# Weight-sum additions moved to VectorE, their splits and the second pair's factors rescheduled

## The chip, the cores and the metric

The kernel runs on one core of a Trainium2 chip. Its time is the device time of one execution in microseconds (us); the times shown are medians of several runs. Beside each timed kernel there is one execution taken by the hardware profiler, and every row in this document comes from such a profile. The engines are TensorE (PE, with its weight loads PEld), VectorE (DVE), ScalarE (ACT), GpSimd (POOL) and SyncE (SP), which issues nearly all transfers between HBM and the on-chip memory. Each engine works through its own queue in order, and an instruction that waits holds up all that stand behind it in that queue.

## The reference

Random-feature attention for 4 batches of 8 heads, 576 positions and head width 64, followed by two feed-forward layers:

```python
def phi(x):
    h = einsum('bhsd,md->bhsm', x, omega) - sum(x * x) / 2
    return exp(h - max(h)) / sqrt(128)
q_p, k_p = phi(q * scale), phi(k * scale)
kv, z = einsum('bhsm,bhsd->bhmd', k_p, v), sum(k_p, axis=2)
x = (q_p @ kv) / (q_p @ z + 1e-6)            # 2304 tokens x 512
h = x @ w_in;  x = (h * clip(h + 3, 0, 6) / 6) @ w_out      # first layer, 512 -> 2048 -> 512
h = x @ w2_in; x = (h * sigmoid(1.702 * h)) @ w2_out        # second layer
```

The feed-forward weights arrive as 64-bit floating-point words.

## The kernel before

Each 32-bit operand of a large product is split into a high and a low half (a copy into the matmul's format on one engine, a subtraction on another), and a product is three matmuls: high by high, high by low, low by high.

The program has four stages.

- Attention of batch 0 (0 to some 60 us), with the conversion of the first layer's weights beside it.
- The first layer, one batch of 512 tokens after the other, each in 16 chunks `c` of 128 hidden features (`emit_h`, `emit_o`, two chunks apart). Between a batch's matmuls stand the attention steps of the next batch, called from `side()`. All 32 weight tiles (16 of `w_in`, 16 of `w_out`) are converted during batch 0. `HELD` of them stay on the chip; the others are stored to HBM and fetched again in each of the later three batches, through six buffers `wss`, two chunks ahead (`AHEAD`).
- From batch 1 to the ninth chunk of batch 3 (205 to 505 us) the second layer's weights are converted and summed. The list `late` holds this work for eight pairs `u` of chunks. `convert_1` and `convert_2` make the 32-bit weights `w` of a chunk. The second layer uses a scheme of seven block products in place of eight, for which sums of quarter blocks of the weights are needed. `sums` makes them in place, four additions for `w_in` and four for `w_out` of each pair, and `put_sums` splits eight halves of the blocks into `wsn` tiles (a copy on ScalarE, L216, a subtraction on GpSimd, L217) and stores each tile to HBM (`sums_dram`, `left_dram`).
- The second layer (from 575 us) in two pairs `p` of batches. `h_pair` makes the gated values `g` of 256 hidden features, eight times for a pair; `o_pair` multiplies them with `w_out` in seven products of eight turns `u`. In each turn `halves` splits a value (ScalarE L954, VectorE L955) into one of three `gs` tiles and 12 matmuls follow (L960); `total` adds blocks of `g` on GpSimd (L944 to L950). The factors of the next pair, `x_ops`, are made beside the first pair's `o_pair`: two loads and 14 steps that split a block (ScalarE L636, VectorE L637) and add one on GpSimd (L624 to L630), called from that loop's own `side()`.

What stands where in an engine's queue is not fixed by the order of the code. A scheduler runs through the program ahead of time with its own model of how long each instruction takes. It places an instruction when its inputs and its buffer are there, and the place in the code decides only between instructions that are ready together.

Of the kernel before, what the change touches and what calls it, by code (L numbers as in the profile page):

```python
# [22 lines left out]
def performer_moe_kernel(  # L23
# [34 lines left out]
    HELD = 9  # L58
# [155 lines left out]
    def put_sums(u, kind, t):  # L214
        s = wp.tile([P, 2, 2, DM // 2], F32R, tag="wsn", bufs=2, name="wsn")
        nc.scalar.copy(s[:, :, 0], t)  # L216
        nc.gpsimd.tensor_tensor(out=s[:, :, 1], in0=t, in1=s[:, :, 0].bitcast(F32), op=ALU.subtract)  # L217
        if kind in "abcd":
            to = sums_dram[u, kind]
        else:  # L220
            k = LEFT.index(kind)
            to = left_dram[:, k:k + 2, u].rearrange("p o (s d) -> p o s d", s=2)
        nc.sync.dma_start(out=to, in_=s.bitcast(F32))

    def sums(u, k, step):
        w0, w1 = whole[2 * u][:, k], whole[2 * u + 1][:, k]
        first, second = (("a", "b"), ("c", "d")) if k == 0 else (("11", "12"), ("s4", "s2"))
        if step == 0:
            put_sums(u, first[0], w0)
            put_sums(u, first[1], w1)  # L230
            return
        sub = dict(op=ALU.subtract)
        a11, a22 = w0[:, 0], w1[:, 1]
        a12, a21 = (w0[:, 1], w1[:, 0]) if k == 0 else (w1[:, 0], w0[:, 1])
        nc.gpsimd.tensor_tensor(out=a22, in0=a21, in1=a22, op=ALU.add)
        nc.gpsimd.tensor_tensor(out=a21, in0=a11, in1=a21, **sub)
        nc.gpsimd.tensor_tensor(out=a11, in0=a22, in1=a11, **sub)
        nc.gpsimd.tensor_tensor(out=a12, in0=a12, in1=a11, **sub)  # L238
        put_sums(u, second[0], w1)
        put_sums(u, second[1], w0)  # L240
# [250 lines left out]
    def emit_h(n, c, side):  # L491
        w = ws[0, "i", c].rearrange("p s (k f) -> p s k f", k=NK)
        for i, N in SEGS[n]:
# [26 lines left out]
            if i == n:  # L520
                after_gate()
# [185 lines left out]
    for u in range(NC // 2):  # L707
        late += [
            (True, lambda u=u: convert_next(1, NC + 2 * u + 1, *gate)),
            (True, lambda u=u: convert_next(1, NC + 2 * u + 2, *gate)),  # L710
            (False, lambda u=u: convert_next(2, NC + 2 * u + 1)),
            (False, lambda u=u: convert_next(2, NC + 2 * u + 2)),
        ] + [(False, lambda u=u, k=k, j=j: sums(u, k, j)) for k in range(2) for j in range(2)]
    slots = (B - 2) * NC + PREP
    n_late = [0, 0]

    def before_chunk(n, c):
        n_late[1] = min(len(late), -(-len(late) * ((n - 1) * NC + c + 1) // slots))
        while n_late[0] < n_late[1] and not late[n_late[0]][0]:
            late[n_late[0]][1]()  # L720
            n_late[0] += 1

    def after_gate():
        while n_late[0] < n_late[1]:
            late[n_late[0]][1]()
            n_late[0] += 1
# [27 lines left out]
    def side():  # L754
        pace[1] += 1
        if pace[1] % 2:
            return
# [33 lines left out]
    for u in range(len(units) + LAG):  # L791
        while fetches and fetches[0][0] <= u + AHEAD:
            fetch_w(0, *fetches.pop(0)[1:])
        if u < len(units):
# [21 lines left out]
            if n == B - 1 and c >= PREP:  # L816
                if c == PREP:
# [242 lines left out]
    for p in range(B // 2):  # L1060
        while prep:
            prep.pop(0)()
        for u in range(NC // 2):
            h_pair(p, u)
# [70 lines left out]
```

## Time and profile before

| | |
|---|---|
| median of 3 runs | 961.22 us (959.08 to 962.56) |
| profiled execution, whole | 962.68 us |
| its span, first to last instruction | 960.9 us |
| TensorE busy | 925.2 us (96%) |
| VectorE busy | 617.0 us (64%) |
| ScalarE busy | 481.4 us (50%) |
| GpSimd busy | 410.9 us (43%) |
| moved between HBM and the chip | 211.97 MB |
| mean granted TensorE clock | 0.998 of full speed |

The busy time of an engine is the time in which at least one of its instructions ran. A matmul's end is modelled, so that a short stand of TensorE between two matmuls can hide in it.

### The profile page before, as it was taken

What the parts mean: (1) busy time and instruction counts of PE and PEld (TensorE: products, weight loads), DVE (VectorE), ACT (ScalarE), POOL (GpSimd) and SP (SyncE); (2) the same over time, 40 slices, a digit from 0 to 9 for tenths busy, and PEclk for the clock granted to TensorE, in tenths of its full rate; (3) what the DMA queues carried; (4) which work ended last, traced back from release to release, by engine and by line L of the source; (5) the groups of instructions that cost most, each with busy time, mean ns of one, the idle gap of its engine ahead of it and who ended that gap; (6) DMA issues with size and microseconds to landing.
All of it is one profiled execution on the core that took longest, in us unless ns stands there. A gap on an engine that the chain in (4) does not pass through costs nothing.

```text
span 960.9 us, 16331 instructions
## 1 busy us (share of the span) xinstructions
PE 925.2 (96%) x6238; PEld 788.5 (82%) x6238; DVE 617.0 (64%) x946; ACT 481.4 (50%) x977; POOL 410.9 (43%) x335
## 2 busy tenths in 40 slices
PE   8899999999999999999999999997899999999997
PEld 7777777778877877878888887886899888889997
DVE  6888899588574866656627244439976443477743
ACT  5887676576554765645534234334444232244443
POOL 0122213068564466646654006658822254464400
PEclk9999999999999999999999999999999999999999
DMA  5668678678888687876665247765467555555572
GB/s 176 224 230 282 203 260 308 239 278 304 308 295 288 231 285 275 293 264 211 228 242 175 88 133 252 227 209 189 152 190 227 190 165 171 175 175 163 172 259 88
DMA packets 70558, 211.97 MB, mean 221 GB/s; under 512 B 6992, under 2 KB 12752, under 8 KB 70480
## 3 DMA queue, kind: packets, MB, share of 16 engines
q1 hardware_dynamic: 70320, 210.67, 65.0%
q8 instruction: 49, 0.80, 0.3%
q10 hardware_dynamic: 160, 0.26, 0.1%
q14 instruction: 29, 0.24, 0.1%
HBM read 155.85 MB, written 55.05 MB: 219 GB/s over the span
## 4 chain that ended last, share of the span: by engine, by line
PE 50%; DVE 20%; POOL 10%; ACT 8%; DMA 7%; issue 4%; POOLq 0%; SPq 0%; ACTq 0%; DVEq 0%
PE o L960 16%; PE h L844 15%; PE o L550 6%; PE ps L500 6%; DVE w L202 4%; POOL wsn L217 4%; DMA sumsd<-wsn 3%; DVE gs L955 2%; PE hl L861 2%; POOL w L195 2%; DVE xo L637 2%; DVE wtop L186 2%; ACT wsn L216 2%; DVE gs L517 2%; ACT e L263 2%
## 5 line engine op out<-in xcount | busy, mean ns | idle before, releaser
L960 PE MATMUL o<-wss,gs 128*128 128x256 f32 x1536 | 192.2, 285 | 12.2 <-DVE gs L955 12.1
L960 PEld LDWEIGHTS o<-wss,gs 128*128 128x128 f32 x1536 | 187.8, 192 | 16.9 <-DVE gs L955 16.2
L195 POOL TENSOR_TENSOR w<-w,wpow 128x512 f32<-128x512 f32 x64 | 77.2, 1228 | 201.5 <-DVE wpow L190 128.7
L844 PE MATMUL h<-xo,wss 128*128 128x512 f32 x672 | 160.8, 393 | 0.1
L550 PE MATMUL o<-gs,wss 128*128 128x512 f32 (+1 forms) x660 | 150.5, 375 | 1.5 <-ACT gs L516 1.5
L500 PE MATMUL ps<-x,wss 128*128 128x512 f32 x576 | 146.8, 398 | 5.1 <-DVE ga L512 2.5
L844 PEld LDWEIGHTS h<-xo,wss 128*128 128x128 f32 x672 | 124.1, 188 | 26.7 <-DMA wss<-sumsa 0.5
L955 DVE TENSOR_TENSOR gs<-g,gs 128x512 fp32r<-128x512 f32 x112 | 114.8, 1047 | 46.2 <-ACT gs L954 45.4
L550 PEld LDWEIGHTS o<-gs,wss 128*128 128x128 f32 x660 | 112.2, 188 | 22.5 <-ACT gs L516 2.9
L500 PEld LDWEIGHTS ps<-x,wss 128*128 128x128 f32 x576 | 104.1, 188 | 30.1 <-DVE ga L512 3.2
L954 ACT CAST gs<-g 128x512 fp32r<-128x512 f32 x112 | 69.6, 621 | 94.2 <-PE o L960 87.1
L217 POOL TENSOR_TENSOR wsn<-w,wsn 128x512 fp32r<-128x512 f32 x64 | 89.0, 1395 | 62.4 <-ACT wsn L216 62.4
L885 POOL TENSOR_TENSOR g<-g,c 128x512 f32<-128x512 f32 x48 | 64.2, 1338 | 102.5 <-ACT g L884 101.9
L512 DVE SCALAR_TENSOR_TENSOR ga<-ga,ps 128x512 f32<-128x512 f32 (+1 forms) x80 | 49.7, 628 | 84.5 <-ACT ga L511 84.2
L202 DVE TENSOR_TENSOR w<-w,wtop 128x512 f32<-128x512 f32 x64 | 71.6, 1131 | 21.8 <-POOL w L195 21.3
L216 ACT CAST wsn<-w 128x512 fp32r<-128x512 f32 x64 | 39.7, 624 | 81.2 <-POOL w L238 26.8
L517 DVE TENSOR_TENSOR gs<-ga,gs 128x512 fp32r<-128x512 f32 (+1 forms) x80 | 64.0, 812 | 24.5 <-ACT gs L516 23.7
L511 ACT ACTIVATE ga<-ps,three 128x512 f32<-128x512 f32 (+1 forms) x80 | 51.5, 650 | 47.4 <-PE ps L500 47.3
L263 ACT ACTIVATE e<-ps,mx 128x128 f32<-128x128 f32 x220 | 62.9, 395 | 23.1 <-DVE mx L261 22.9
L884 ACT ACTIVATE g<-c 128x512 f32<-128x512 f32 x48 | 30.4, 633 | 79.8 <-DVE c L877 79.8
L550 PE MATMUL o<-gs,wsh 128*128 128x512 f32 (+1 forms) x300 | 68.9, 376 | 1.2 <-ACT gs L516 1.2
L550 PEld LDWEIGHTS o<-gs,wsh 128*128 128x128 f32 x300 | 51.4, 188 | 11.2 <-ACT gs L516 1.5
(158 smaller groups left out, 1356.0 us busy)
## 6 DMA issues: line engine op xcount, KB each, us to landing
wss<-left SPq DMA_DIRECT2D x64, 512.0 KB, 3.7
wss<-ws0i SPq DMA_DIRECT2D x36, 512.0 KB, 4.5
wss<-ws0o SPq DMA_DIRECT2D x33, 512.0 KB, 4.5
wraw<-in_w_in_dram SPq DMA_DIRECT2D x32, 512.0 KB, 4.9
wraw<-in_w_out_dram SPq DMA_DIRECT2D x32, 512.0 KB, 5.8
left<-wsn SPq DMA_DIRECT2D x32, 512.0 KB, 3.2
wss<-sumsa SPq DMA_DIRECT2D x16, 512.0 KB, 3.3
wss<-sumsd SPq DMA_DIRECT2D x16, 512.0 KB, 4.1
```

Source lines behind the costliest of these rows:

```text
L195: nc.gpsimd.tensor_tensor(out=w[:, cols], in0=w[:, cols], in1=q[:, cols], op=ALU.mult)
L202: nc.vector.tensor_tensor(out=wj, in0=wj, in1=a[:, j * DM:(j + 1) * DM], op=ALU.add)
L217: nc.gpsimd.tensor_tensor(out=s[:, :, 1], in0=t, in1=s[:, :, 0].bitcast(F32), op=ALU.subtract)
L263: act = nc.scalar.activation(out=e[:, r, :], in_=ps[:, r, :], func=AF.Exp, bias=mx[:, r:r + 1])
L500: nc.tensor.matmul(out=ps, lhsT=w[:, wi, kk, :], rhs=x[:, xi, kk, :], start=(m == 0), stop=(m == 3 * NK - 1),)
L517: gate[1] = nc.vector.tensor_tensor(out=s[:, 1, :], in0=g, in1=s[:, 0, :].bitcast(F32), op=ALU.subtract)
L550: nc.tensor.matmul(out=ps[:, e, :], lhsT=w[:, wi, cols], rhs=s[:, gi, :], start=(c == 0 and m == 0 and per == 1), stop=(c == NC - 1 and m ...
L844: nc.tensor.matmul(out=ps, lhsT=s[:, wi, q, :], rhs=xop[q, op][:, xi], start=(first and m == 0), stop=(m == 5), skip_group_check=not first,)
L885: eng.tensor_tensor(out=g, in0=g, in1=src, op=ALU.mult)
L954: nc.scalar.copy(s[:, 0], g)
L955: nc.vector.tensor_tensor(out=s[:, 1], in0=g, in1=s[:, 0].bitcast(F32), op=ALU.subtract)
L960: nc.tensor.matmul(out=out, lhsT=s[:, gi, d * P:(d + 1) * P], rhs=w[:, wi, :], start=(start and m == 0), stop=(stop and m == 2), skip_grou ...
```

## The change

Four things are edited.

- `HELD` goes from 9 to 8. The tiles that stay are now eight of `w_out`; before they were four of `w_in` and five of `w_out`. A third `wsn` tile takes the room.
- `sums` is cut into eight calls per pair, one split each, called one at a time from `side()`; before, they were four calls ahead of a chunk. The order of the eight splits changes with it.
- The four additions of each block go from GpSimd to VectorE.
- In the second layer the second pair's factors are paced over 48 turns, from the seventh on, and the first three splits of `o_pair`'s first product are made inside the last `h_pair`, ahead of its last product.

```diff
-    HELD = 9
+    HELD = 8
...
-    def put_sums(u, kind, t):
-        s = wp.tile([P, 2, 2, DM // 2], F32R, tag="wsn", bufs=2, name="wsn")
+    def put_sums(u, k, i):
+        kind = (("a", "b", "c", "d"), ("11", "12", "s4", "s2"))[k][i]
+        t = whole[2 * u + (i in (1, 2))][:, k]
+        s = wp.tile([P, 2, 2, DM // 2], F32R, tag="wsn", bufs=3, name="wsn")
         nc.scalar.copy(s[:, :, 0], t)
         nc.gpsimd.tensor_tensor(out=s[:, :, 1], in0=t, in1=s[:, :, 0].bitcast(F32), op=ALU.subtract)
...
-        nc.gpsimd.tensor_tensor(out=a22, in0=a21, in1=a22, op=ALU.add)
-        nc.gpsimd.tensor_tensor(out=a21, in0=a11, in1=a21, **sub)
-        nc.gpsimd.tensor_tensor(out=a11, in0=a22, in1=a11, **sub)
-        nc.gpsimd.tensor_tensor(out=a12, in0=a12, in1=a11, **sub)
-        put_sums(u, second[0], w1)
-        put_sums(u, second[1], w0)
+        nc.vector.tensor_tensor(out=a22, in0=a21, in1=a22, op=ALU.add)
+        nc.vector.tensor_tensor(out=a21, in0=a11, in1=a21, op=ALU.subtract)
+        nc.vector.tensor_tensor(out=a11, in0=a22, in1=a11, op=ALU.subtract)
+        nc.vector.tensor_tensor(out=a12, in0=a12, in1=a11, op=ALU.subtract)
+
+    def sums(u, n):
+
+        k, i = ((0, 0), (0, 1), (1, 0), (1, 1), (0, 2), (0, 3), (1, 2), (1, 3))[n]
+        put_sums(u, k, i)
+        if n in (2, 4):
+            add_sums(u, n // 2 - 1)
...
-        ] + [(False, lambda u=u, k=k, j=j: sums(u, k, j)) for k in range(2) for j in range(2)]
+        ] + [("side", lambda u=u, n=n: sums(u, n)) for n in range(8)]
...
         if pace[1] % 2:
+            late_at("side", 1)
             return
...
         gated(3, c22, nc.gpsimd)
+        first_split()
         product(4, "b", 1, b7, False)
...
-                s = halves(gp, SM, quarters(u)[src])
+                s = ready.pop(0) if op == 1 and ready else halves(gp, SM, quarters(u)[src])
...
+    def split_early():
+        ready.extend(halves(gp, SM, gt[u, 0][:, 0]) for u in range(3))
...
-            h_pair(p, u)
+            h_pair(p, u, split_early if u == NC // 2 - 1 else lambda: None)
...
-        wait = [2]
+        turn = [0, len(prep)]
 
         def side():
-            wait[0] -= 1
-            if prep and wait[0] < 0:
+            turn[0] += 1
+            while prep and (turn[0] - 6) * turn[1] > (turn[1] - len(prep)) * 48:
                 prep.pop(0)()
```

Three places show what the scheduler makes of it. The numbers behind a name tell its buffers apart, and the lines of the changed kernel are a few further down the file.

ScalarE before, around the sums of the first pair of chunks (`w_2295` and `w_2309`): L216 is the copy that begins a split, L511 and L516 belong to the first layer's gating, L263 are the attention's exponentials.

```order
L516 CAST gs_2489<-ga_2486 128x512 [waits DVE_49]
L216 CAST wsn_2469<-w_2309 128x2x256 [waits DVE_49,Activation_49]
L511 ACTIVATE ga_2569<-ps_2556,three_86 128x512 [waits PE_49]
L516 CAST gs_2572<-ga_2569 128x512 [waits DVE_49]
L368 COPY kv_2586<-ps_2575 128x65 [waits PE_49]
L216 CAST wsn_2540<-w_2309 128x2x256 [waits DMAHW3_49,Activation_49,Pool_49]
L263 ACTIVATE e_2595<-ps_2588,mx_2596 128x128 [waits DVE_49]
L263 ACTIVATE e_2595<-ps_2588,mx_2596 128x128 x3
L263 ACTIVATE e_2595<-ps_2614,mx_2621 128x128 [waits DVE_49]
L263 ACTIVATE e_2595<-ps_2614,mx_2621 128x128 x3
L216 CAST wsn_2544<-w_2295 128x2x256 [waits DMAHW6_49,Activation_49,Pool_49]
```

ScalarE in the changed kernel, the same place (L218 the copy of a split, L512, L517 and L264 the others).

```order
L517 CAST gs_2491<-ga_2488 128x512 [waits DVE_49]
L218 CAST wsn_2478<-w_2311 128x2x256 [waits DVE_49,Activation_49]
L218 CAST wsn_2508<-w_2297 128x2x256
L512 ACTIVATE ga_2563<-ps_2546,three_86 128x512 [waits PE_49]
L218 CAST wsn_2553<-w_2311 128x2x256 [waits DMAHW4_49,DVE_49,Pool_49]
L517 CAST gs_2566<-ga_2563 128x512 [waits DVE_49]
L369 COPY kv_2580<-ps_2569 128x65 [waits PE_49]
L264 ACTIVATE e_2589<-ps_2582,mx_2590 128x128 [waits DVE_49]
L264 ACTIVATE e_2589<-ps_2582,mx_2590 128x128 x3
L264 ACTIVATE e_2589<-ps_2616,mx_2623 128x128 [waits DVE_49]
L264 ACTIVATE e_2589<-ps_2616,mx_2623 128x128 x2
L218 CAST wsn_2602<-w_2311 128x2x256 [waits DMAHW7_49,Pool_49]
```

Ahead of the two groups of exponentials three copies stand in place of two, and the first two of them back to back.

VectorE before, the same place in the program: L512 and L517 are the gating, L261 the maximum of the attention's features, L312 and L313 a split of its inputs.

```order
L517 TENSOR_TENSOR gs_2489<-ga_2486,gs_2489 128x512 [waits Activation_49]
L512 SCALAR_TENSOR_TENSOR ga_2569<-ga_2569,ps_2556 128x512 [waits Activation_49]
L517 TENSOR_TENSOR gs_2572<-ga_2569,gs_2572 128x512 [waits Activation_49]
L261 TENSOR_REDUCE mx_2596<-ps_2588 128x4 [waits PE_49]
L312 CAST thi_2813<-qk_2770 128x512 [waits PE_49]
L261 TENSOR_REDUCE mx_2621<-ps_2614 128x4 [waits PE_49]
L313 TENSOR_TENSOR tlo_2814<-qk_2770,thi_2813 128x512 [waits DVE_49]
L512 SCALAR_TENSOR_TENSOR ga_2658<-ga_2658,ps_2645 128x512 [waits Activation_49]
L517 TENSOR_TENSOR gs_2661<-ga_2658,gs_2661 128x512 [waits Activation_49]
```

VectorE in the changed kernel (L231 to L234 the additions, L513 and L518 the gating, L262 the maximum).

```order
L518 TENSOR_TENSOR gs_2491<-ga_2488,gs_2491 128x512 [waits Activation_49]
L513 SCALAR_TENSOR_TENSOR ga_2563<-ga_2563,ps_2546 128x512 [waits Activation_49]
L231 TENSOR_TENSOR w_2311<-w_2311 128x256 [waits Pool_49]
L232 TENSOR_TENSOR w_2311<-w_2297,w_2311 128x256 [waits DVE_49]
L233 TENSOR_TENSOR w_2297<-w_2311,w_2297 128x256 [waits DVE_49]
L518 TENSOR_TENSOR gs_2566<-ga_2563,gs_2566 128x512 [waits Activation_49]
L234 TENSOR_TENSOR w_2297<-w_2297 128x256 [waits DVE_49]
L262 TENSOR_REDUCE mx_2590<-ps_2582 128x4 [waits PE_49]
L231 TENSOR_TENSOR w_2311<-w_2297,w_2311 128x256 [waits Pool_49]
L313 CAST thi_2815<-qk_2772 128x512 [waits DMAHW6_49,PE_49]
L262 TENSOR_REDUCE mx_2623<-ps_2616 128x4 [waits PE_49]
L232 TENSOR_TENSOR w_2297<-w_2297 128x256 [waits DVE_49]
```

The additions stand between the gating and the maxima; the first of each four waits for GpSimd, the others for the one before.

VectorE before, at the end of the first pair's last `h_pair` and the start of `o_pair`: L955 are splits of gated values, L637 the second pair's factors, L877 the additions of `h_pair`.

```order
L955 TENSOR_TENSOR gs<-g,gs 128x512
L877 TENSOR_TENSOR c_7000<-u_6963,h 128x512
L637 TENSOR_TENSOR xo<-xr,xo 128x512 x4
L877 TENSOR_TENSOR c_7015<-u_6963,h 128x512
L955 TENSOR_TENSOR gs<-g,gs 128x512
L637 TENSOR_TENSOR xo<-xr,xo 128x512
L955 TENSOR_TENSOR gs<-g,gs 128x512 x2
L637 TENSOR_TENSOR xo<-xr,xo 128x512
L955 TENSOR_TENSOR gs<-g,gs 128x512
L637 TENSOR_TENSOR xo<-xr,xo 128x512
L955 TENSOR_TENSOR gs<-g,gs 128x512 x2
L637 TENSOR_TENSOR xo<-xr,xo 128x512 x2
```

VectorE in the changed kernel, the same place (L940 the splits, L638 the factors, L879 the additions).

```order
L940 TENSOR_TENSOR gs<-g,gs 128x512
L879 TENSOR_TENSOR c_7008<-u_6971,h 128x512
L638 TENSOR_TENSOR xo<-xr,xo 128x512 x4
L879 TENSOR_TENSOR c_7032<-u_6971,h 128x512
L940 TENSOR_TENSOR gs<-g,gs 128x512
L638 TENSOR_TENSOR xo<-xr,xo 128x512
L940 TENSOR_TENSOR gs<-g,gs 128x512 x2
L638 TENSOR_TENSOR xo<-xr,xo 128x512
L940 TENSOR_TENSOR gs<-g,gs 128x512
L638 TENSOR_TENSOR xo<-xr,xo 128x512
L940 TENSOR_TENSOR gs<-g,gs 128x512 x2
L638 TENSOR_TENSOR xo<-xr,xo 128x512 x2
```

Nothing moved here: the rows follow one another as before, in spite of the other place in the code, and so do all rows of all engines from the second layer's first matmul on.

## Rows read from the trace of the kernel before

**Rows 1.** The page: busy time of each engine, share of the span, instructions.

```profile
PE 925.2 (96%) x6238; PEld 788.5 (82%) x6238; DVE 617.0 (64%) x946; ACT 481.4 (50%) x977; POOL 410.9 (43%) x335
```

**Rows 2.** Busy time of each engine by stretch: columns as in the first line.

```profile
core 0: us, PE busy (x) PEld busy (x) DVE busy (x) ACT busy (x) POOL busy (x), PEclk, DMA share, GB/s
...
205.00:505.00 300.00, 295.56 (x1975) 241.61 (x1975) 185.60 (x304) 167.97 (x356) 178.24 (x159) 1.00 0.77 271
...
650.00:700.00 50.00, 39.44 (x286) 36.88 (x286) 47.24 (x38) 23.55 (x41) 39.90 (x25) 0.97 0.51 167
...
850.00:961.00 111.00, 103.83 (x851) 101.83 (x849) 73.10 (x88) 45.45 (x83) 36.53 (x24) 0.99 0.56 173
```

**Rows 3.** TensorE waits, 650 to 700 and 850 to 961 us: total, times, longest.

```profile
PE o L960 <- DVE gs L955: 10.5, 6, 2.5
...
PE o L960 <- DVE gs L955: 1.6, 2, 1.0
```

**Rows 4.** Waits of TensorE, 205 to 505 us.

```profile
PE ps L374 <- ACT e L263: 2.0, 2, 1.2
PE ps L500 <- DVE ga L512: 1.2, 2, 0.9
PE ps L255 <- DVE xln L415: 0.4, 1, 0.4
PE ps L500 <- ACT qtl L308: 0.4, 1, 0.4
```

**Rows 5.** Timeline, 278 to 290 us: start, length, instruction, idle before and releaser.

```profile
285.50 0.62 ACT L216 CAST wsn<-w 128x512 fp32r<-128x512 f32 x1 [1.24 <-DMA sumsc<-wsn]
...
287.48 2.79 PE L500 MATMUL ps<-x,wss 128*128 128x512 f32 x11 [0.94 <-DVE ga L512]
```

**Rows 6.** Timeline, 338 to 343 us.

```profile
339.01 0.62 ACT L216 CAST wsn<-w 128x512 fp32r<-128x512 f32 x1 [3.16 <-DMA sumsc<-wsn]
...
341.28 0.69 DVE L512 SCALAR_TENSOR_TENSOR ga<-ga,ps 128x512 f32<-128x512 f32 x1 [4.25 <-ACT ga L511]
...
341.78 1.43 PE L500 MATMUL ps<-x,wss 128*128 128x512 f32 x5 [0.40 <-ACT qtl L308]
```

**Rows 7.** Timeline, 404 to 413.5 us.

```profile
410.94 0.62 ACT L216 CAST wsn<-w 128x512 fp32r<-128x512 f32 x1 [3.69 <-DMA sumsd<-wsn]
...
412.65 0.66 PE L374 MATMUL ps<-ident,e 128*128 128x128 f32 x4 [1.20 <-ACT e L263]
```

**Rows 8.** Timeline, 346 to 356 us.

```profile
354.54 0.66 PE L374 MATMUL ps<-ident,e 128*128 128x128 f32 x4 [0.84 <-ACT e L263]
```

**Rows 9.** Waits of ScalarE, 205 to 505 us.

```profile
ACT wsn L216 <- POOL w L238: 26.8, 14, 3.9
...
ACT wsn L216 <- DMA sumsd<-wsn: 15.0, 7, 3.7
...
ACT wsn L216 <- DMA sumsc<-wsn: 6.5, 5, 3.2
```

**Rows 10.** DMA issues: KB of each, median us to landing.

```profile
wss<-ws0i SPq DMA_DIRECT2D x36, 512.0 KB, 4.5
```

**Rows 11.** GpSimd by line, 205 to 505 us: busy us, mean ns, idle.

```profile
L217 POOL TENSOR_TENSOR wsn<-w,wsn 128x512 fp32r<-128x512 f32 x63 | 87.5, 1394 | 62.4 <-ACT wsn L216 62.4
...
L236 POOL TENSOR_TENSOR w<-w 128x256 f32<-128x256 f32 x16 | 14.1, 881 | 1.3
...
L238 POOL TENSOR_TENSOR w<-w 128x256 f32<-128x256 f32 x16 | 12.7, 793 | 0.9
```

**Rows 12.** VectorE's groups: whole span, 205 to 505 us, 660 to 690 us.

```profile
L206 DVE TENSOR_TENSOR wss<-w,wss 128x512 fp32r<-128x512 f32 x23 | 15.5, 682 | 0.3
...
L202 DVE TENSOR_TENSOR w<-w,wtop 128x512 f32<-128x512 f32 x29 | 32.6, 1141 | 10.9 <-POOL w L195 10.6
...
L637 DVE TENSOR_TENSOR xo<-xr,xo 128x512 fp32r<-128x512 f32 x7 | 12.4, 1775 | 0.0
```

**Rows 13.** Waits of VectorE, 205 to 505 us.

```profile
DVE ga L512 <- ACT ga L511: 58.8, 24, 4.6
```

More of the change, by code (lines that the diff above doesn't have):

```diff
@@ L520, in emit_h @@
             if i == n:
-                after_gate()
+                late_at("gate")
             hgt[i, c] = s
@@ L708, in performer_moe_kernel, with late_at @@
         late += [
[L709 to L712, printed above, removed]
-        ] + [(False, lambda u=u, k=k, j=j: sums(u, k, j)) for k in range(2) for j in range(2)]
+            ("gate", lambda u=u: convert_next(1, NC + 2 * u + 1, *gate)),
+            ("gate", lambda u=u: convert_next(1, NC + 2 * u + 2, *gate)),
+            ("chunk", lambda u=u: convert_next(2, NC + 2 * u + 1)),
+            ("chunk", lambda u=u: convert_next(2, NC + 2 * u + 2)),
+        ] + [("side", lambda u=u, n=n: sums(u, n)) for n in range(8)]
     slots = (B - 2) * NC + PREP
     n_late = [0, 0]
+    def late_at(place, most=None):
+        while n_late[0] < n_late[1] and late[n_late[0]][0] == place and most != 0:
+            late[n_late[0]][1]()
+            n_late[0] += 1
+            most = most and most - 1
     def before_chunk(n, c):
         n_late[1] = min(len(late), -(-len(late) * ((n - 1) * NC + c + 1) // slots))
[L719 to L726, printed above, removed]
+        late_at("chunk")
     xblk[0] = new_x(0)
@@ L817, in performer_moe_kernel @@
                 if c == PREP:
+                    assert n_late[0] == len(late), (n_late, len(late))
                     prep = x_ops(0, wp, "w")
@@ L832, in performer_moe_kernel, with h_pair @@
     l1 = ctx.enter_context(tc.tile_pool(name="l1", bufs=1, reuse_waits="tile"))
-    def h_pair(p, u):
+    def h_pair(p, u, first_split):
         psum, tag, oth, otag = (acc, "acc", psp, "ps") if u % 2 else (psp, "ps", acc, "acc")
@@ L930, in performer_moe_kernel, with halves @@
     gl = {}
+    ready = []
+    def halves(pool, N, g):
+        s = pool.tile([P, 2, N], F32R, tag="gs", bufs=3, name="gs")
+        nc.scalar.copy(s[:, 0], g)
+        nc.vector.tensor_tensor(out=s[:, 1], in0=g, in1=s[:, 0].bitcast(F32), op=ALU.subtract)
+        return s
     def o_pair(p, side):
@@ L950, in total @@
                 add(out=b21, in0=b21, in1=b11, op=ALU.subtract)
-        def halves(pool, N, g):
-            s = pool.tile([P, 2, N], F32R, tag="gs", bufs=3, name="gs")
-            nc.scalar.copy(s[:, 0], g)
-            nc.vector.tensor_tensor(out=s[:, 1], in0=g, in1=s[:, 0].bitcast(F32), op=ALU.subtract)
-            return s
         def rows(s, w, out, d, start, stop, fresh):
```

14 lines of the change are left out of this document (4 added, 10 removed).

## Prediction

> **What bounds the kernel now.** First the page's busy times: TensorE is busy 96% of the span, VectorE 64%, GpSimd 43% [rows 1]. An engine that full can only be sped up where it stands still, so the next view is the busy time by stretch [rows 2]. The weight sums are made between 205 and 505 us; there TensorE is busy 295.56 of 300 us, so it stands for 4.4 us in all. The first second-layer product over the gated values begins at 650 us, and between 650 and 700 us TensorE works 39.4 of 50 us: 10.6 us lost, the largest hole of the kernel. From 850 us on, where the second pair's such product begins, it is 103.8 of 111, most of which is the tail after the last matmul.
>
> Then the waits of TensorE. In the hole at 650 us it waits for one thing only, the low half of a split value on VectorE (L955): 10.5 us in 6 waits. At 850 us, the same code without the other pair's factors beside it costs 1.6 us in 2 waits [rows 3]. In the weight-sum stretch there are six named waits, 4.0 us in all: for exponentials, for gated values, for two copies [rows 4].
>
> The reader should now ask what was late behind those six. Three times the timeline shows ScalarE standing in front of a split of a weight sum (L216) until the store of an earlier split had landed and its tile was free, with TensorE's wait right behind it. At 285.50 it had waited 1.24 us and TensorE then stood 0.94 us [rows 5]; at 339.01 it had waited 3.16 us, and TensorE stood 0.40 us [rows 6]; at 410.94 it had waited 3.69 us, and TensorE stood 1.20 us [rows 7]. That is 0.94 + 0.40 + 1.20 = 2.5 us of the 4.4. A fourth, 0.84 us at 354.54 [rows 8], lies behind another cause: ScalarE has a weight conversion between the exponentials there. In total ScalarE stands 21.5 us for stores of two kinds of sums and 26.8 us for GpSimd's last addition [rows 9].
>
> **The change part by part.**
>
> *The second pair's factors and the early splits.* In the code both move: the 17 steps of the factors from one step per turn to the 48 turns that begin with the seventh, the first three splits ahead of the last product that makes gated values. The order of instructions says that nothing moves. A scheduler places each instruction once its inputs and buffers are there, and where the code writes it matters only between instructions that compete. VectorE's rows around the first product stand as before, the factors (L637, now L638) between the same splits (L955, now L940); so do all rows of every engine from the first second-layer matmul on. Price: 0. What the edit would be worth if it did spread the factors is 10.5 - 1.6 = 8.9 us [rows 3]; that is a rival below.
>
> *One first-layer tile fewer held.* One more store and three more fetches of 512 KB, at 4.5 us to landing [rows 10]. Fetches are issued two chunks ahead, and not one of the six waits in the stretch ends with the landing of such a tile [rows 4]. Price: 0, covered by the two-chunk lead. If the cover were gone for all three, 3 x 4.5 = 13.5 us.
>
> *A third tile for the splits.* It gives each split one more split's time before ScalarE must stand for a landing. At most it returns the 2.5 us above, at least nothing, since the new order also puts the casts nearer to each other (in ScalarE's rows two casts of a pair now stand back to back), and so leaves less time between a store and the next use of its tile. I take 1.5 us: two of the three waits were preceded by stands of 3 us and more, of which one split more (cast and subtraction, 0.62 us [rows 5] and 1.39 us [rows 11]) takes away some six tenths; 2.5 x 0.6 is 1.5.
>
> *The additions on VectorE.* 64 additions of 128x256 leave GpSimd: four lines of 16, each of 12.7 to 14.1 us, some 53 us [rows 11]. On VectorE no row shows one. From below, half of a 128x512 subtraction in SBUF without company, 682/2 = 341 ns, makes 22 us; from above, half of the 1775 ns that such a subtraction takes beside a busy GpSimd makes 57 us; the addition of the conversion in this very stretch, 1141/2 = 570 ns, makes 37 us [rows 12]. I take 37: it is the same stretch, with the same neighbours. VectorE then has 185.6 + 37 = 223 of 300 us [rows 2], so it is not the bound, and the work lies beside TensorE's. It reaches TensorE only through what queues behind it: the gating (L512, L517) and the maxima of the attention.
>
> *The new wait.* The first addition of each of 16 sets waits for a split on GpSimd to have read its input, and with it wait the rows behind it on VectorE. One split is 1.39 us [rows 11], so 16 x 1.39 = 22 us at most if each set stands for a whole one. How much of that TensorE feels can be read: in this stretch VectorE already stands 58.8 us in 24 waits at L512 [rows 13], and TensorE lost 1.2 us to L512 [rows 4], a fiftieth. At 341.28 L512 had stood 4.25 us, and TensorE stood 0.40 us around it [rows 6]. By the fiftieth, the 37 + 22 us cost TensorE 1.2 us; since additions that fall into VectorE's 114 idle us delay nothing, I take half, 0.6 us. From below it is 0; from above, each of the 16 sets costs the 0.40 us of that one place: 6.4 us.
>
> *Sum.* 0 + 0 - 1.5 + 0.6 = -0.9 us. The profiled execution took 962.68 us, of which 960.9 is the span; it lies 1.46 us above the median of the three timed runs, 961.22. So 961.8 for it, and **960.3 us** against the median. What a measurement of this kernel can tell from no change is about 0.3%, 2.9 us.
>
> **The rivals.**
>
> *All standing in the weight-sum stretch goes (faster).* For it: casts, gating and exponentials share ScalarE's queue, so a free split helps all of them, and GpSimd's 53 us less leave VectorE's two-operand work alone more often. Against it: the 0.84 us at 354.54 is not the splits' [rows 8], and the new order makes new neighbours. 961.2 - 4.4 = 956.8 us. Chance 0.17.
>
> *The factors do get spread (faster).* It would take an order on the chip other than the one that I read. 961.2 - 8.9 - 0.9 = 951.4 us. Chance 0.03.
>
> *VectorE falls behind in bursts (slower).* The eight additions of a pair stand within some thirty rows of VectorE's queue, and GpSimd's splits run through the same time. In the hole at 650 us just this is seen: VectorE busy 47.2 of 50 us with GpSimd busy 39.9, its subtractions at 1775 ns where 682 is their own length [rows 2, 12]. The Trainium skill has a rule for it ("SBUF — State Buffer", section "Who interferes with whom"): a VectorE instruction with two SBUF inputs and a GpSimd instruction that reads SBUF exclude each other, and the second one waits for the whole first. The trace agrees in size, 1775 - 682 = 1093 ns for one such wait. Worked out from rows: an addition that meets a split would take up to 341 + 1093 = 1434 ns, and 64 of them 92 us, which fills VectorE to 278 of 300. Then each of the 16 sets costs TensorE its 0.40 us [rows 6], and more where two sets meet: 6.4 - 1.5 = +4.9, 966.1 us. It decides where a set makes L512 more than about 4 us late, which is what TensorE took with 0.40 us. Against it: GpSimd itself has 53 us less to do in the same stretch, so there are fewer meetings, not more. Chance 0.11.
>
> *A fetch comes late (slower).* With every input tile streamed, six buffers turn over three tiles in two chunks. If one fetch in each of the three later passes were late by its whole landing, 961.2 + 13.5 - 0.9 = 973.8 us. Against it: no wait of TensorE ends with a landing now. Chance 0.03.
>
> **How the numbers follow.** The forecast, a change of between -2.9 and +2.9 us, has 0.66: its own range runs from 961.2 - 2.5 = 958.7 us, where all of the landings' price comes back and the additions cost nothing, to 962.4, where nothing comes back and VectorE's 59 us cost their full fiftieth. Faster has 0.17 + 0.03 = 0.20, slower 0.11 + 0.03 = 0.14. The range goes down to the first rival, 956.6, and up into the third, 964.8; outside lie the second and fourth rival (0.06), the upper half of the third and the lower edge of the first.
>
> **What would show it.** Right: TensorE's waits at L960 between 650 and 700 us are again about 10.5 us; ScalarE's stands before the splits for landings fall clearly below 21.5 us; VectorE's busy time in 205 to 505 us grows by 20 to 57 us and GpSimd's falls by some 50; TensorE stands there between 2 and 5 us. Wrong: a first product without its hole (then the order read here is not what ran), a TensorE wait that ends with a streamed tile, or VectorE's additions with stands of several us in front of them and L512 late behind, with TensorE's standing in the stretch above 7 us.

## The result and the profile after

| | before | after |
|---|---|---|
| median | 961.22 us (959.08 to 962.56) | 966.03 us (965.45 to 966.86) |
| profiled execution, its span | 962.68, 960.9 us | 966.03, 964.2 us |
| first matmul of the second layer | 574.6 us | 577.9 us |

The ratio of the times is 1.0055, with a 95% interval of 1.0039 to 1.0071. So the changed kernel is slower by 3.7 to 6.8 us. The forecast was 960.3 us, with 0.66 on no measurable change; what came is 1.2 us above the upper end of the range, 964.8, and within 0.1 us of the third rival's 966.1, which the range left out.

The first view to read is where each kernel's second layer begins. It begins 3.3 us later, and the span is 3.3 us longer: from there to the end both take 386.3 us. The whole loss lies ahead of it. Its size is taken from the medians, since single executions of the same code differ here by some 2 us: with the second layer's edits alone, whose first part is that of the kernel before, the second layer begins at 572.4 us.

Busy time of each engine by stretch, the changed kernel (it answers to [rows 2]; the columns are in the first line):

```profile
core 0: us, PE busy (x) PEld busy (x) DVE busy (x) ACT busy (x) POOL busy (x), PEclk, DMA share, GB/s
205.00:505.00 300.00, 290.40 (x1928) 236.93 (x1927) 226.84 (x366) 166.60 (x353) 127.59 (x95) 1.00 0.77 271
650.00:700.00 50.00, 38.16 (x274) 34.86 (x273) 46.51 (x37) 22.34 (x39) 42.56 (x27) 1.00 0.55 172
```

In the stretch of the weight sums TensorE stands for 300 - 290.4 = 9.6 us, where it stood for 4.4. (Up to the second layer's first matmul it stands 22.7 us, where it stood for 18.0. It is also busy 1.5 us less in this execution, and so the start moves by only 3.3.) VectorE has 41 us more to do, GpSimd 51 us less. The hole at 650 us is there as before; TensorE's waits at the low halves between 640 and 760 us [rows 3] are now:

```profile
PE o L965 <- DVE gs L940: 11.8, 7, 2.5
```

What TensorE waits for between 205 and 505 us, the changed kernel (it answers to [rows 4]: total, times, longest):

```profile
PE ps L256 <- DVE ga L513: 2.5, 3, 1.2
PE ps L375 <- ACT e L264: 1.9, 3, 1.3
PE ps L501 <- DVE ga L513: 1.5, 4, 0.6
PE ps L256 <- DVE llo L314: 1.3, 1, 1.3
PE o L551 <- DVE ob L580: 1.0, 1, 1.0
...
```

The gating on VectorE (L513, L512 before) costs 4.0 us in 7 waits, where it cost 1.2 in 2 [rows 4]. Two more waits are for VectorE too, and the exponentials (L264) wait for its maxima. ScalarE's waits in the same stretch, the changed kernel, say the same: VectorE is late.

```profile
...
ACT gs L517 <- DVE ga L513: 25.6, 25, 2.8
ACT e L264 <- DVE mx L262: 23.5, 14, 3.5
...
ACT wsn L218 <- DMA sumsc<-wsn: 2.8, 2, 2.0
...
ACT wsn L218 <- DMA sumsa<-wsn: 2.4, 4, 1.2
```

The first two were 8.5 and 14.8 us before. The stands for landings, 21.5 us in two rows before [rows 9], are down to 5.2, as was expected of the third tile.

Now the additions themselves. The single lines of the changed kernel, all in the weight-sum stretch (shortest, median and longest in ns, then first and last start):

```profile
L231 DVE TENSOR_TENSOR w<-w x16: 410/1500/1534, 206.6 to 491.0; 128x256 f32<-128x256 f32 x16
...
  POOL wsn L219: 1.6, 2
...
L232 DVE TENSOR_TENSOR w<-w x16: 411/902/1424, 207.6 to 493.1; 128x256 f32<-128x256 f32 x16
...
L233 DVE TENSOR_TENSOR w<-w x16: 406/425/1516, 209.0 to 493.7; 128x256 f32<-128x256 f32 x16
...
L234 DVE TENSOR_TENSOR w<-w x16: 409/426/1512, 209.9 to 494.2; 128x256 f32<-128x256 f32 x16
```

Most additions take some 420 ns. 25 of the 64, 13 of them the first of a set, take between 0.76 and 1.53 us, and by the timeline a split of GpSimd is under way when each of the 25 begins; the 35 that no GpSimd instruction overlaps take 406 to 427 ns. The wait in front of the first addition of a set is next to nothing (1.6 us in 2 waits); the time is inside the additions. The four lines are busy 18.9 + 14.5 + 9.9 + 7.8 = 51.1 us. At 0.42 each they would be 26.9, so some 24 us of them are standing.

One set on the timeline of the changed kernel (start, length, instruction, idle before it and releaser):

```profile
240.88 4.40 POOL L219 TENSOR_TENSOR wsn<-w,wsn 128x512 fp32r<-128x512 f32 x3 [4.62 <-ACT wsn L218]
...
242.65 1.50 DVE L231 TENSOR_TENSOR w<-w 128x256 f32<-128x256 f32 x1
...
242.97 0.69 ACT L512 ACTIVATE ga<-ps,three 128x512 f32<-128x512 f32 x1
...
244.18 1.39 DVE L232 TENSOR_TENSOR w<-w 128x256 f32<-128x256 f32 x1
...
245.60 0.42 DVE L233 TENSOR_TENSOR w<-w 128x256 f32<-128x256 f32 x1
246.06 0.43 DVE L234 TENSOR_TENSOR w<-w 128x256 f32<-128x256 f32 x1
...
246.48 0.68 DVE L513 SCALAR_TENSOR_TENSOR ga<-ga,ps 128x512 f32<-128x512 f32 x1
...
247.19 0.62 ACT L517 CAST gs<-ga 128x512 fp32r<-128x512 f32 x1 [2.42 <-DVE ga L513]
247.21 0.19 PEld L256 LDWEIGHTS ps<-bd_hi,thi 128*128 128x128 f32 x1 [0.92 <-DVE ga L513]
247.21 0.39 PE L256 MATMUL ps<-bd_hi,thi 128*128 128x256 f32 x1 [0.78 <-DVE ga L513]
```

GpSimd runs three splits back to back until 245.28. The two additions that start before that take 1.50 and 1.39 us, the two after it 0.42 and 0.43. The gating's input was ready at 242.97 + 0.69 = 243.66; it starts 2.8 us later, and TensorE stands 0.78 us.

This is the theory that the runs test: **the new order of splits has a further split ready on GpSimd when the additions are released, the additions meet it, VectorE falls behind, and the gating with it.** Its rivals: the new order itself costs the time; VectorE's load as such; the new wait; the third tile with its streamed weights; the second layer's edits.

### The profile page after: what moved, and what is told of

It is laid out like the page before. It is cut to its first block, busy times and chain, and to the rows that moved or that the text cites. A ratio compares the mean times of both kernels' runs of the same rounds, so it can differ in the third digit from the quotient of the medians.

```text
span 964.2 us, 16360 instructions
## 1 busy us (share of the span) xinstructions
PE 922.5 (96%) x6238; PEld 785.4 (81%) x6238; DVE 659.7 (68%) x1010; ACT 481.2 (50%) x977; POOL 361.1 (37%) x271
## 4 chain that ended last, share of the span: by engine, by line
PE 48%; DVE 12%; ACT 3%; issue 2%; DMA 2%; POOL 1%; SPq 0%; DVEq 0%; POOLq 0%
PE o L965 16%; PE h L846 16%; PE o L551 6%; PE ps L501 5%; DVE gs L940 2%; PE hl L863 2%; DVE xo L638 2%; DMA xr<-xs 2%; DVE w L202 1%; DVE gs L518 1%; DVE w L231 1%; POOL w L195 1%; DVE ga L513 1%; DVE w L232 1%; PE ps L256 1%
## 5 line engine op out<-in xcount | busy, mean ns | idle before, releaser
L965 PEld LDWEIGHTS o<-wss,gs 128*128 128x128 f32 x1536 | 186.3, 191 | 18.4 <-DVE gs L940 17.7
L501 PE MATMUL ps<-x,wss 128*128 128x512 f32 x768 | 194.0, 397 | 5.2 <-DVE ga L513 1.5
L501 PEld LDWEIGHTS ps<-x,wss 128*128 128x128 f32 x768 | 139.3, 188 | 38.0 <-ACT wss L205 3.0
L940 DVE TENSOR_TENSOR gs<-g,gs 128x512 fp32r<-128x512 f32 x112 | 114.7, 1047 | 45.8 <-ACT gs L939 45.2
L219 POOL TENSOR_TENSOR wsn<-w,wsn 128x512 fp32r<-128x512 f32 x64 | 91.0, 1436 | 69.7 <-ACT wsn L218 63.4
L551 PE MATMUL o<-gs,wsh 128*128 128x512 f32 (+1 forms) x480 | 111.8, 377 | 1.2 <-DVE ob L580 1.0
L551 PE MATMUL o<-gs,wss 128*128 128x512 f32 (+1 forms) x480 | 109.6, 374 | 2.4 <-ACT gs L517 2.4
L551 PEld LDWEIGHTS o<-gs,wss 128*128 128x128 f32 x480 | 81.7, 188 | 17.5 <-ACT gs L517 3.4
L551 PEld LDWEIGHTS o<-gs,wsh 128*128 128x128 f32 x480 | 81.7, 188 | 17.4 <-DVE ob L580 1.2
L513 DVE SCALAR_TENSOR_TENSOR ga<-ga,ps 128x512 f32<-128x512 f32 (+1 forms) x80 | 49.8, 627 | 59.4 <-ACT ga L512 59.0
L512 ACT ACTIVATE ga<-ps,three 128x512 f32<-128x512 f32 (+1 forms) x80 | 51.7, 653 | 67.9 <-PE ps L501 67.9
L264 ACT ACTIVATE e<-ps,mx 128x128 f32<-128x128 f32 x220 | 62.8, 394 | 31.7 <-DVE mx L262 31.5
L202 DVE TENSOR_TENSOR w<-w,wtop 128x512 f32<-128x512 f32 x64 | 68.1, 1073 | 12.5 <-POOL w L195 12.0
L518 DVE TENSOR_TENSOR gs<-ga,gs 128x512 fp32r<-128x512 f32 (+1 forms) x80 | 63.3, 802 | 13.3 <-ACT gs L517 11.9
L517 ACT CAST gs<-ga 128x512 fp32r<-128x512 f32 (+1 forms) x80 | 45.7, 581 | 30.9 <-DVE ga L513 30.7
```

The costliest lines, as they stand in the source:

```text
L202: nc.vector.tensor_tensor(out=wj, in0=wj, in1=a[:, j * DM:(j + 1) * DM], op=ALU.add)
L264: act = nc.scalar.activation(out=e[:, r, :], in_=ps[:, r, :], func=AF.Exp, bias=mx[:, r:r + 1])
L501: nc.tensor.matmul(out=ps, lhsT=w[:, wi, kk, :], rhs=x[:, xi, kk, :], start=(m == 0), stop=(m == 3 * NK - 1),)
L518: gate[1] = nc.vector.tensor_tensor(out=s[:, 1, :], in0=g, in1=s[:, 0, :].bitcast(F32), op=ALU.subtract)
L551: nc.tensor.matmul(out=ps[:, e, :], lhsT=w[:, wi, cols], rhs=s[:, gi, :], start=(c == 0 and m == 0 and per == 1), stop=(c == NC - 1 and m ...
L940: nc.vector.tensor_tensor(out=s[:, 1], in0=g, in1=s[:, 0].bitcast(F32), op=ALU.subtract)
```

## The experiments

All ratios are to the kernel before, run beside them (its medians were 959.9 to 960.4 us there), with 95% intervals. The table has the numbers that the runs are compared by (205 to 505 us: TensorE's standing time, which is 300 less its busy time, and VectorE's busy time).

| kernel | median, us | ratio | TensorE stands | VectorE busy |
|---|---|---|---|---|
| the change | 966.03 | 1.0055 (1.0039 to 1.0071) | 9.6 | 226.8 |
| additions back on GpSimd | 958.05 | 0.9987 (0.9977 to 0.9997) | 2.9 | 193.2 |
| before, additions on VectorE | 959.98 | 1.0001 (0.9991 to 1.0010) | 5.1 | 204.6 |
| before, third tile | 957.30 | 0.9971 (0.9960 to 0.9982) | 2.4 | 190.4 |
| before, second layer's edits | 960.67 | 1.0008 (0.9995 to 1.0022) | 3.6 | 187.7 |
| before, third tile and VectorE | 960.58 | 1.0004 (0.9990 to 1.0017) | 3.3 | 210.3 |
| the change, splits that read nothing | 953.90 | 0.9940 (0.9919 to 0.9960) | 0.1 | 195.5 |
| the change, splits behind the additions | 957.84 | 0.9974 (0.9964 to 0.9984) | 1.9 | 214.7 |
| the change, old order of splits | 959.20 | 0.9993 (0.9979 to 1.0008) | 4.3 | 211.7 |
| third tile, factors held over 48 turns | 954.36 | 0.9940 (0.9919 to 0.9960) | 3.1 | 189.8 |
| third tile, factors held over 28 turns | 951.54 | 0.9907 (0.9890 to 0.9923) | 3.0 | 189.8 |
| the change, factors held over 28 turns | 960.60 | 1.0005 (0.9995 to 1.0015) | 9.6 | 226.5 |
| the change with both repairs | 952.85 | 0.9918 (0.9903 to 0.9933) | 3.0 | 212.9 |

### The parts of the change, one at a time

**The change with its additions back on GpSimd.** All four lines of `add_sums`:

```diff
-        nc.vector.tensor_tensor(out=a22, in0=a21, in1=a22, op=ALU.add)
+        nc.gpsimd.tensor_tensor(out=a22, in0=a21, in1=a22, op=ALU.add)
```

> The changed kernel with its 64 additions back on GpSimd, all else as changed. Theory (the additions on VectorE meet GpSimd's splits, and what queues behind them on VectorE makes TensorE stand): VectorE's busy time between 205 and 505 us falls from 227 to about 186 us, TensorE's standing there from 9.6 to 3 to 4.5 us, and the time to 959.5 to 961.5 us. Rival 1 (the eight splits one behind the other, in their new order and from three tiles, are what crowds ScalarE and the stores): the time stays at 965 to 967 us. Rival 2 (the streamed tile): the same, 965 to 967 us, with waits of TensorE that end with a landing.

0.9987: the loss is gone, and a little is won. VectorE is busy 193 us, somewhat more than expected. The tile, the streamed weights, the new order and the second layer's edits together do not cost the time; the additions' place does, by 1.0055 - 0.9987 = 0.0068, or 6.5 us. The two kernels were not run beside each other; by the two intervals it is some 5 to 8 us.

**The kernel before, with its additions on VectorE.** The same four lines, the other way round, two tiles and the old order.

> The kernel before with its 64 additions on VectorE and nothing else changed. Theory: the whole loss comes with it, 965 to 968 us, since ScalarE's stands for landings stay and VectorE's lateness is added; the first addition of each four takes about 1.5 us. Rival 1 and rival 2 (order of the splits, streamed tile): 960.5 to 962.5 us, since neither is in it.

1.0001: a miss. The same move costs nothing here. The median of each line is 420 to 426 ns, so these additions run alone almost always, and the wait in front of them is long (first line of this kernel, as above):

```profile
L235 DVE TENSOR_TENSOR w<-w x16: 393/420/426, 207.8 to 491.0; 128x256 f32<-128x256 f32 x16
...
  POOL wsn L217: 13.6, 5
```

So the new wait is not the loss: it is 13.6 us here without one, and 1.6 us in the change. The move alone is not it either. What is left is the move together with the new order or the third tile.

**The kernel before with the third tile and one tile fewer held.**

```diff
-    HELD = 9
+    HELD = 8
...
-        s = wp.tile([P, 2, 2, DM // 2], F32R, tag="wsn", bufs=2, name="wsn")
+        s = wp.tile([P, 2, 2, DM // 2], F32R, tag="wsn", bufs=3, name="wsn")
```

> The kernel before with one held tile fewer and a third tile for the splits, nothing else. Theory: 959 to 961 us; ScalarE's stands in front of the splits for landings fall from 23 us to under 10, and TensorE's standing between 205 and 505 us from 4.4 to 2 to 4 us. Rival 2 (the streamed tile costs): 963 us or more, with a wait of TensorE or of ScalarE that ends with a fetched tile.

0.9971, 1.7 to 3.8 us faster, somewhat more than expected. No wait of TensorE in the stretch ends with a streamed tile.

**The kernel before with the second layer's edits alone** (the new pacing of the factors and the three early splits, as in the change's diff).

> The kernel before with the two edits of the second layer alone (the pacing of the second pair's factors, the early splits). The order of instructions is that of the kernel before on every engine. Theory: no difference, 960 to 962.5 us, and the hole between 650 and 700 us with 10 to 12 us of TensorE's waiting for the low halves. Rival (the edits do act, and for the worse or the better): more than 2 us from 961.2 on either side.

1.0008, not to be told from none; TensorE's wait in the hole is 11.8 us in 7 waits.

**The third tile and the additions on VectorE together, old order.** The edits of the second and third run in one kernel.

> The kernel before with a third split tile, one held tile fewer and the additions on VectorE, but the splits in their old order: behind the second split of a pair GpSimd has nothing to do until VectorE has added. Theory (what costs is that in the new order a further split is ready on GpSimd just when the additions are released, so that they wait for the whole of it): the additions take 410 to 430 ns each, the gain of the third tile stays, 0.996 to 0.9985 of the kernel before. Rival (a third tile and additions on VectorE do not go together, whatever the order): 1.003 to 1.006, as with the whole change.

1.0004: between the two expectations. The additions are short (422 to 426 ns in the median), and the loss of the change is not there. But the third tile's 0.0029 is not kept. TensorE stands 3.3 us in the stretch, 1.9 of it one wait for VectorE's division (L415) at the end of an attention step. Ahead of it on VectorE:

```profile
233.29 3.40 POOL L217 TENSOR_TENSOR wsn<-w,wsn 128x512 fp32r<-128x512 f32 x2
...
233.88 1.70 DVE L517 TENSOR_TENSOR gs<-ga,gs 128x512 fp32r<-128x512 f32 x1
...
235.50 1.75 DVE L202 TENSOR_TENSOR w<-w,wtop 128x512 f32<-128x512 f32 x1
...
237.17 0.28 DVE L415 TENSOR_TENSOR xln<-ps,rden 64x128 f32<-64x128 f32 x1
...
237.50 0.39 PE L255 MATMUL ps<-bd_hi,thi 128*128 128x256 f32 x1 [1.88 <-DVE xln L415]
```

Two other subtractions of VectorE, some 0.68 us at their shortest, take 1.70 and 1.75 us beside two splits. Behind the stretch there is one more wait, 2.9 us for the gating at 513.75 us, which is 0.3 us with the third tile alone:

```profile
PE ps L500 <- DVE ga L512: 2.9, 1, 2.9
```

Up to the second layer's first matmul TensorE stands 18.4 us here and 15.3 us there, and these two waits are enough to make up that difference.

### The meeting itself

**The change, with splits that do not read.** GpSimd fills the low half of each weight-sum split with zeros in place of the subtraction, so the low halves of the second layer's weights are left out:

```diff
-        nc.gpsimd.tensor_tensor(out=s[:, :, 1], in0=t, in1=s[:, :, 0].bitcast(F32), op=ALU.subtract)
+        nc.gpsimd.memset(s[:, :, 1].bitcast(F32), 0.0)
```

> The changed kernel in which GpSimd, for the low half of each weight-sum split, fills the tile with zeros in place of subtracting, so that it reads nothing there; the low halves of the second layer's weights are left out. Theory (an addition waits for a GpSimd instruction that reads the same memory): the first addition of four falls from 1500 to about 420 ns, VectorE's busy time in 205 to 505 us by 20 to 30 us, and the time to 0.995 to 0.999 of the kernel before. Rival (the additions stand in VectorE's queue at the wrong places, whatever GpSimd does): the time stays above 1.003.

0.9940, better than expected, and the stretch has next to no standing time left. The additions and what GpSimd does beside them (the split's line, as above; the fill takes 527 ns):

```profile
L231 DVE TENSOR_TENSOR w<-w x16: 406/414/427, 203.5 to 473.9; 128x256 f32<-128x256 f32 x16
...
L219 POOL MEMSET wsn<- x64: 516/527/840, 0.9 to 481.4; 128x512 f32 x64
```

The additions are as short as alone. The Trainium skill's page "SBUF — State Buffer" (section "Who interferes with whom") says that a VectorE instruction with two SBUF inputs contends with a GpSimd instruction that reads SBUF, and not with one that only writes it. The trace agrees: 18 of the 64 additions run beside a fill and take 409 to 427 ns, and none of the 64 is longer than 429 ns. But this run takes away more than the meetings with the additions. GpSimd has 51 us less to do, and VectorE's other subtractions are shorter too (L518: 665 ns in the mean, 858 in the change). It shows the cause to be possible, and does not size it.

**The change, with no split beside the additions.** GpSimd does all its work, but a write of one column by VectorE, behind the last addition, stands in the tiles of the next splits, so that they begin after the set:

```diff
         nc.scalar.copy(s[:, :, 0], t)
+        if (k, i) in ((1, 0), (1, 1), (0, 2)):
+            with behind(last_add[0]):
+                nc.vector.memset(s[:, 0, 1, 0:1].bitcast(F32), 0.0)
...
-        nc.vector.tensor_tensor(out=a12, in0=a12, in1=a11, op=ALU.subtract)
+        last_add[0] = nc.vector.tensor_tensor(out=a12, in0=a12, in1=a11, op=ALU.subtract)
...
-        put_sums(u, k, i)
         if n in (2, 4):
             add_sums(u, n // 2 - 1)
+        put_sums(u, k, i)
```

> The changed kernel with its new order of splits and its additions on VectorE; added is a write of one column by VectorE behind the last addition of each set into the tiles of the next two or three splits, so that GpSimd cannot begin one of these splits while the set's additions run (GpSimd's work is the same, only later). Theory (the loss is the meeting of an addition with the split that GpSimd has ready behind the release): the additions take 410 to 430 ns in the median, also at the first two lines, where the change has 1500 and 902; VectorE is busy 200 to 212 us between 205 and 505 us (226.8 in the change); TensorE stands there 3 to 6 us (9.6 in the change); ratio 0.998 to 1.001. Rival (the new order of splits, or work moved to VectorE as such, costs the time): the additions become short, but the ratio stays at 1.003 to 1.007 and TensorE stands 8 us or more.

0.9974, a little better than expected (VectorE's 214.7 us lie above the 212): the whole loss is gone and the third tile's gain is there, with the change's order of splits (in three of the eight pairs c and d change places), the same engine for the additions and 24 writes of one column more. The two lines that were 1500 and 902 ns in the median, and GpSimd's waits in front of its splits:

```profile
L236 DVE TENSOR_TENSOR w<-w x16: 407/414/427, 206.5 to 483.7; 128x256 f32<-128x256 f32 x16
...
  POOL wsn L224: 7.3, 6
...
L237 DVE TENSOR_TENSOR w<-w x16: 407/425/428, 207.0 to 484.6; 128x256 f32<-128x256 f32 x16
...
  DVE wsn L223: 29.0, 10
```

GpSimd now stands 29 us for VectorE, and nobody feels it. VectorE stands 7.3 us in front of the first additions, more than the 1.6 of the change, and that costs nothing either. The timeline of this kernel at the same place of the program as that of the change above:

```profile
242.10 0.41 DVE L236 TENSOR_TENSOR w<-w 128x256 f32<-128x256 f32 x1
242.55 0.42 DVE L237 TENSOR_TENSOR w<-w 128x256 f32<-128x256 f32 x1
243.01 0.42 DVE L238 TENSOR_TENSOR w<-w 128x256 f32<-128x256 f32 x1
243.47 0.42 DVE L239 TENSOR_TENSOR w<-w 128x256 f32<-128x256 f32 x1
...
244.89 0.69 DVE L518 SCALAR_TENSOR_TENSOR ga<-ga,ps 128x512 f32<-128x512 f32 x1 [0.91 <-ACT ga L517]
```

The set takes 1.8 us, not 3.8, and the gating (L518 here) is not late: VectorE stands idle before it, for ScalarE.

**The change with the old order of splits**, one at a time as in the change (a, b, additions, c, d, then the same for the other block):

```diff
-        k, i = ((0, 0), (0, 1), (1, 0), (1, 1), (0, 2), (0, 3), (1, 2), (1, 3))[n]
-        put_sums(u, k, i)
-        if n in (2, 4):
-            add_sums(u, n // 2 - 1)
+        k, i = ((0, 0), (0, 1), (0, 2), (0, 3), (1, 0), (1, 1), (1, 2), (1, 3))[n]
+        if n in (2, 6):
+            add_sums(u, k)
+        put_sums(u, k, i)
```

> The changed kernel with three tiles, one split at a time and additions on VectorE, but with the old order of a pair's splits: a, b, additions, c, d, then 11, 12, additions, s4, s2. Now the additions are released when no further split is ready on GpSimd but those that wait for the additions themselves. Theory of the meetings: additions 410 to 430 ns in the median at all four lines, VectorE busy 204 to 214 us between 205 and 505 us, ratio 0.997 to 1.002. Rival (handing out the splits one at a time at the places between chunks costs the time, whatever their order): ratio 1.003 to 1.007 with short additions.

0.9993, with medians of 422 to 426 ns: in the old order the next splits need the additions' results, so GpSimd has none ready at the release. Handing the splits out one at a time is not the loss. What this order adds is on ScalarE, whose casts stand 13.8 and 7.6 us for the second and the fourth addition.

### What the second layer's edit would be worth

The prediction priced the pacing at nothing, since the order of instructions does not change, and said what it would be worth if it did. Here an order edge holds each step of the factors behind the split of its turn, on ScalarE and VectorE. To the kernel with the third tile alone:

```diff
+            mark[:] = (
+                nc.scalar.copy(s[:, 0], g),
+                nc.vector.tensor_tensor(out=s[:, 1], in0=g, in1=s[:, 0].bitcast(F32), op=ALU.subtract),
+            )
...
+            turn[0] += 1
+            while prep and (turn[0] - 6) * turn[1] > (turn[1] - len(prep)) * 48:
+                with behind(mark[0]), behind(mark[1]):
+                    prep.pop(0)()
```

> The kernel before with the third tile (0.9971 by itself), and the second pair's factors really held back: each step may only stand behind the split of the turn in which the code calls it, 17 steps over 48 turns from the seventh on. Theory (the hole at 650 us is the factors crowding VectorE beside GpSimd's additions): TensorE's waits for low halves fall from 11.8 to 3 to 6 us and the time to 0.988 to 0.993. Rival (the hole is made by GpSimd's own additions and stays without the factors): 0.996 to 0.998.

0.9940, 0.0031 better than the third tile alone, and less than expected. The waits at the low halves between 640 and 760 us are 8.3 us in 6, down from 11.8: steps still stand among the first turns' splits.

**The same over 28 turns from the 25th on** (24 and 28 in place of 6 and 48).

> As the run before it, but the 17 steps only from the 25th turn on, over 28 turns, when the first three products with GpSimd's additions are done. Theory: the waits fall to 1.5 to 3 us, as in the second pair's product, and the time to 0.986 to 0.990. Rival (the factors are then late for the next pair's first products): a wait at the start of the second pair's gated values, and no more than 0.995.

0.9907, the fastest kernel here, if not quite what was expected (4.7 us of waits for 1.5 to 3). TensorE is busy 49.2 of the 50 us from 650 on, where it was 38.2 with the third tile alone. Its remaining waits at the low halves (640 to 760 us):

```profile
PE o L963 <- DVE gs L957: 4.7, 6, 1.3
```

**The change with the factors held over 28 turns.** The same edge in the changed kernel.

> The changed kernel with the second pair's factors really held behind the splits of the turn, 17 steps over 28 turns from the 25th on, everything else as in the change. If the hole of the second layer and the weight sums' loss are apart from each other, the gain of this holding (0.9907 against 0.9971 with the third tile alone, so 0.0064) adds to the change's 1.0055: ratio 0.998 to 1.0005, waits at the low halves between 640 and 760 us 4 to 6 us. Rival (the loss between 205 and 505 us is made up of the same slack of VectorE that the holding uses): ratio 1.002 or more.

1.0005: the holding is worth 0.0050 here, 0.0064 above. The two stretches are apart: TensorE still stands 9.6 us in the weight sums.

**The change with both repairs**, splits behind the additions and factors held.

> The changed kernel with both repairs: no split of GpSimd beside the additions of its set, and the second pair's factors held behind the splits of the turn, 17 steps over 28 turns from the 25th on. If each repair acts on a stretch of its own, the ratio is 0.9974 less the 0.0050 to 0.0064 that the holding was worth in the other two kernels: 0.990 to 0.993; TensorE stands under 3 us between 205 and 505 us and waits 4 to 6 us at the low halves. Rival (the two share VectorE's slack): 0.994 or more.

0.9918, 7.5 us under the kernel before, as the two repairs added up. It is not told from the kernel with the third tile and held factors (0.9907), so the move to VectorE, once mended, is worth nothing that could be measured.

## Why the prediction was wrong

**What failed: the additions on VectorE with the new wait, +0.6 us taken.** They cost about 6.5 us (5 to 8), at the upper bound of 6.4. The step had three parts, and the runs tell them apart.

- *VectorE's load, 37 us taken, 22 to 57 given.* It grew by 41 us. This was right as a growth; the additions themselves took 51.1 us and VectorE's other work 10 less.
- *The new wait, up to 22 us.* It is 1.6 us in the change, and harmless where it is larger: 13.6, 7.3 and 10.3 us (additions on VectorE alone, splits held behind, old order), in three kernels that are not slower. This was wrong in what it looked for.
- *TensorE's share, a fiftieth of what VectorE is delayed, halved.* This is the step that failed. Against the same kernel with its additions on GpSimd, VectorE has 226.8 - 193.2 = 33.6 us more and TensorE stands 9.6 - 2.9 = 6.7 us more: a fifth. The fiftieth was read from VectorE's own stands [rows 13], which are slack: VectorE waits there for ScalarE. So is the 0.40 us a set of the upper bound: at that place VectorE stood idle for 4.25 us, and TensorE's wait ended with a copy of ScalarE [rows 6]. The work added here came in bursts of up to 4 us at the moment when a gating is due.

**The rival that came true, VectorE falling behind in bursts (966.1 us, 0.11).** Its mechanism is shown: splits held behind the additions take the loss away, with the engine of the additions and GpSimd's work as in the change. That its size came out was luck. It let all 64 additions meet a split, 92 us in all; they take 51.1, and 25 of them met one. So there were four tenths of the meetings, each of them dearer to TensorE, and the 0.40 us a set was no reading of lateness. The sum came out the same: 6.5 us where it had 6.4, and -1.2 us for the other edits (0.9987) where it had -1.5.

**Why it had only 0.11.** The argument against it was that GpSimd has 53 us less to do, so there are fewer meetings. GpSimd did get 51 us less, and the meetings came all the same. How busy GpSimd is does not say when it is busy. In the new order the next two splits of a set need nothing from the additions, so GpSimd can go on to them at the release; in the old one the next splits need the additions. The order of instructions, which could be read beforehand, says so. In the trace of the change 13 of the 16 first additions meet a split. Two of the 13 stood until GpSimd ended one split and began as it took up the next (276.01 and 487.24 us); the other eleven followed other work of VectorE, as in the set above, and found a later split under way. In the three kernels with the old order and the additions on VectorE no first addition met one.

**What was right.** The second layer's edits at 0: both layers take 386.3 us from the first matmul to the end, and alone they measure 1.0008. The streamed tile at 0: alone with the third tile the kernel is faster. Of the signs of being right, the hole, the landings and the loads of VectorE and GpSimd came; TensorE's standing, 9.6 us for 2 to 5, did not. The hole at 650 us worth up to 8.9 us: held, the factors gave 0.0064, 6.1 us, and the waits at the low halves fell from 11.8 to 4.7 us. **A size that was off:** the third tile, -1.5 taken with 2.5 as the most; alone it gives 2.8 us (1.7 to 3.8), so all of the landings' price may come back. That the landings set this price is not shown: with the splits held behind the additions, ScalarE stands 24.2 us for landings of all kinds again (23.0 before), and that kernel is no slower (0.9974).

**What stays open.** With the additions on VectorE in the old order the third tile's gain is not seen (1.0004 against 0.9971, and 0.9993 with one split at a time). The additions are short there. A single wait of 1.9 us for VectorE's division is in both traces, and in the first one the later wait of 2.9 us; VectorE's longer subtractions beside the splits stand ahead of the division in both. (With the splits held behind the additions the division stands ahead of the second of them, and TensorE does not wait.) That other work of VectorE meets the splits there is read from the timeline; no run takes these meetings away alone. ScalarE's casts that stand for additions are a rival that was not tried. The new order with the additions on GpSimd is 0.0016 above the third tile alone, with intervals that overlap.

## What to carry to other kernels

When an instruction moves from GpSimd to VectorE, don't count how busy GpSimd is; look at what stands next in GpSimd's queue at the instant that releases the moved instruction. If it is ready and reads SBUF, expect meetings: here 13 of 16 first additions met a split, and a met addition took up to 3.6 times its length. Where it depended on the moved instruction, or was made to, the loss was gone. And before a new pacing in the code is believed, read the order of instructions: here it changed nothing until an order edge held it.

## What the runs showed of the hardware

- A 128x256 VectorE addition with both inputs in SBUF takes 407 to 429 ns where no GpSimd subtraction is under way when it begins (the splits held behind the additions). It takes up to 1534 ns when it begins while GpSimd runs a 128x512 subtraction (1319 ns in the median). VectorE pays for nearly all of it: GpSimd's splits are 1319 ns in the median in the change and 1300 ns with the splits held behind the additions.
- A GpSimd fill of 128x512 (527 ns) beside the same additions adds nothing to them: 409 to 427 ns in 18 of them.
